# Folding a weight by slices of 120 columns instead of 128, in a linear-attention and gated-unit kernel

## The chip, the cores and the metric

The kernel runs on one core of one Trainium2 chip. The metric is the device time of one execution in microseconds. A profile of one execution comes with each kernel; its times count from the start of the span that the profiler saw.

## What is computed

For 2048 tokens of 640 features, the output is the input plus two branches that both read the normalized input:

```python
xn = layernorm(x)                                    # x: 1 x 2048 x 640
# branch A: linear attention, 32 heads of 20
q, k, v = split(xn @ wqkv)                           # wqkv: 640 x 1920
pq, pk = q @ w_phi[h], k @ w_phi[h]                  # w_phi: 32 x 20 x 20
phi_q = concat(softmax(pq), softmax(-pq))            # likewise phi_k
kv, z = phi_k^T v, sum over tokens of phi_k
a = (phi_q kv / (phi_q z + 1e-6)) @ wo
# branch B: gated unit
b = (silu(xn @ w1) * (xn @ w3)) @ w2                 # w1, w3: 640 x 1536
out = x + a + b
```

Since q @ w_phi = xn @ (wq @ w_phi), the kernel first folds phi into the weights: Wkp = wk @ blockdiag(w_phi), and Wqp = wq @ blockdiag(w_phi). This folding is what the change is about.

## The kernel before

Tokens go in 16 tiles of 128 (T), features in 5 chunks of 128 (DC). The kernel text is not a list of instructions in their final order. Each stage is a generator ("stream") that yields steps: norms, transposes, fold_k, attention (value and key tiles, later the fold of the queries' weights), k_norms, loads, key_values, the query streams, mlps (the gated unit, in 4 blocks of 512 tokens by 12 chunks of 128 hidden features) and outs. A planner, `_Program`, holds a cost for every operation and for every DMA, works out for each stream's next step when it could start, and commits the earliest; ties go by the order of the streams. The order in which it commits the steps is the order on each engine. `commit` holds the costs of DMAs: how long the issuing engine is held (`self.free`) and when the data land (`o.end`). The costs shape the order only, and the waits put into the program are those that the dependencies need. All loads are issued on SyncE (SP), except half of token tile 0, which ScalarE issues.

What matters here:

- `first_loads` issues, in this order: token tiles 0 to 2, wv in two halves, token tile 3, the first third of w1 and w3, phi, the transposed load of wk (640 columns of wqkv into wqkT, 5 chunks of 128), token tiles 4 to 7, tiles 8 to 11.
- `warm_up` lets TensorE multiply zeros at the start, 7 products of 512 columns and 11 of 128.
- `norms` normalizes the token tiles; tiles 0 to 3 are transposed on TensorE, tiles 4 to 15 by transposing DMAs into xnT (`loads`). `loads` also issues the other two thirds of w1 and w3, token tiles 12 to 15 and, after tile 9, the transposed load of wq.
- `block_diag` builds the block-diagonal factor BDc on GpSimd, one product with a mask GM for each chunk. 128 is no multiple of a head's 20, so a chunk holds 7 or 8 heads, of which the first and the last may be cut.
- `fold_mm(which, dc, k)` makes 128 rows of a folded weight: for each of the 5 chunks a product with wqkT as the stationary operand and BDc as the moving one, split where the output passes column 320. The two halves lie in two banks of PSUM, and neighbouring chunks add into the columns of the head that they share. It is evacuated to Wqp or Wkp.
- `attention` runs the value tiles 0 to 3, waits for the fold of wk, and goes on with key tiles and, from tile 4, value tiles. From tile 9 it puts one block of the fold of wq behind each tile.
- Every operation is recorded by a helper, so all of them carry one of two line numbers in the profile (102 for operations, 114 for DMAs). Their tiles tell them apart.

Of the kernel before, what the change touches and what calls it, by code (L numbers as in the profile page):

```python
# [3 lines left out]
ACT = mybir.ActivationFunctionType  # L4
# [5 lines left out]
D = 640  # L10
# [10 lines left out]

ENGINES = ("PE", "ACT", "DVE", "POOL", "SP")
GRAN = 32


def heads_of_chunk(c):
    return (128 * c) // DH, (128 * c + 127) // DH


class _Op:  # L30
# [13 lines left out]
class _Program:  # L44
# [127 lines left out]
    def commit(self, ops):  # L172
        for o in ops:
            o.idx = len(self.ops)
            o.deps = self.find_deps(o)
            t = self.free[o.eng]
            for d in o.deps:
                t = max(t, d.end + 0.07)
            o.start = t
            if o.dma:  # L180
                self.free[o.eng] = t + 0.45
                if "T" == o.part:
                    self.free[o.eng] = t + max(1.3, o.cost / 150e3)
                self.bus = max(self.bus, t + 0.5) + o.cost / (280e3 if o.part else 305e3)
                o.end = self.bus + (1.6 if t < 3.5 else 2.6)
            else:
                o.end = t + o.cost
                self.free[o.eng] = o.end
            self.ops.append(o)
            if o.eng == "POOL" and not o.dma:  # L190
                self.pool = o
            for g in o.reads:
                if isinstance(g, tuple):
                    self.bank.setdefault(g, {})[o.eng] = o
                else:
                    self.last_r.setdefault(g, {})[("dma", o.idx) if o.dma else o.eng] = o
            for g in o.writes:
                if isinstance(g, tuple):
                    self.bank.setdefault(g, {})[o.eng] = o
                else:  # L200
                    self.last_w[g] = o
                    self.last_r.pop(g, None)
# [45 lines left out]
def bass_parallel_sum__linear_kernel_hedgehog__glu_gated_swiglu__prompt_kernel(  # L248
# [29 lines left out]
    def new(name, shape, dtype, offset=None):  # L278
        size = mybir.dt.size(dtype)
        for n in shape[1:]:  # L280
            size *= n
        return P.sbuf(name, shape, dtype, region(size) if offset is None else offset)

    ident = new("ident", [128, 128], bf)
    GM = new("GM", [128, DC, H], bf)
    phi_s = new("phi_s", [128, DC, DH], bf)
    BDc = new("BDc", [128, DC, 8 * DH], bf)
    bst = new("bst", [128, T, 16], f32)
    mv = new("mv", [128, T, 8], f32)
    rstd = new("rstd", [128, T, 8], f32)  # L290
# [36 lines left out]
    oT = new("oT", [128, DC, S], bf, RV)  # L327

    RW = region(12800)
    wqkT = new("wqkT", [128, 2 * DC, D], bf, RW)  # L330
    KVc = new("KVc", [128, H * 21], bf, RW)
    half = new("half", [128, 2, 660], f32, RW + 1408)
    Sq = new("Sq", [128, 4, 72], f32, RW + 6688)
# [53 lines left out]
        copy("ACT" if a <= d else "DVE", o, i, 2 if i.dtype == bf else 1)  # L387

    def memset(eng, o, v):
        P.op(eng, "memset", [o], [], (o, v), cost=0.15 + free(o) / 960)  # L390

    def select(o, base, pattern, cm, cmp, fill):
        P.op("POOL", "affine_select", [o], [o], (),
# [4 lines left out]
    x_t = A_x.rearrange("b (t p) d -> p (b t) d", p=128)  # L398
    out_t = out.rearrange("b (t p) d -> p (b t) d", p=128)
    wqkv_t = A_wqkv.rearrange("(c p) n -> p c n", p=128)  # L400
    phi_t = A_w_phi.rearrange("h d f -> (h d) f").rearrange("(c p) f -> p c f", p=128)
    w1_t = B_w1.rearrange("(c p) f -> p c f", p=128)
    w3_t = B_w3.rearrange("(c p) f -> p c f", p=128)

# [4 lines left out]
    def load_x(a, b):  # L409
        P.dma("SP", x_tok[:, a:b, :], x_t[:, a:b, :])  # L410

    def first_loads():
        def half_wv(a):
            P.dma("SP", wv[:, :, a:a + 320], wqkv_t[:, :, 2 * D + a:2 * D + a + 320])

        P.dma("SP", x_tok[:, 0, 0:320], x_t[:, 0, 0:320])
        P.dma("ACT", x_tok[:, 0, 320:D], x_t[:, 0, 320:D])
        load_x(1, 2)
        load_x(2, 3)
        half_wv(0)  # L420
        half_wv(320)
        load_x(3, 4)
        w13(0, 512)
        P.dma("SP", phi_s[:], phi_t)
        P.dma("SP", wqkT[:, DC:2 * DC, :], A_wqkv[:, D:2 * D], True)
        load_x(4, 8)
        load_x(8, 12)


    def consts():  # L430
        memset("DVE", t1[:, 2, :], 0.0)
        memset("DVE", warm[:], 0.0)
        act(warm[:], warm[:], ACT.Exp)
        memset("POOL", ident[:], 0.0)
        select(ident[:], 0, [[-1, 128]], 1, ALU.not_equal, 1.0)
        memset("POOL", GM[:], 1.0)
        select(GM[:], 0, [[128, DC], [-DH, H]], 1, ALU.is_ge, 0.0)
        select(GM[:], DH, [[-128, DC], [DH, H]], -1, ALU.is_gt, 0.0)
        memset("POOL", mhalf[:], -0.5)

    def consts_late():
# [75 lines left out]


    def block_diag():
        for c in range(DC):  # L520
            h0, h1 = heads_of_chunk(c)
            n = h1 - h0 + 1
            tt("POOL", BDc[:, c, 0:n * DH].rearrange("p (h k) -> p h k", k=DH),
               phi_s[:, c, :].unsqueeze(1).to_broadcast([128, n, DH]),
               GM[:, c, h0:h1 + 1].unsqueeze(2).to_broadcast([128, n, DH]), ALU.mult)

    def fold_mm(which, dc, k):
        first = [True, True]
        for e in range(DC):
            h0, h1 = heads_of_chunk(e)  # L530
            lo, hi = DH * h0, DH * (h1 + 1)
            for q in range(2):
                a, b = max(lo, 320 * q), min(hi, 320 * q + 320)
                if a < b:
                    mm(bank(k + q, b - a, a - 320 * q), wqkT[:, which * DC + e, 128 * dc:128 * dc + 128],
                       BDc[:, e, a - lo:b - lo], first[q], e == DC - 1 or (q == 0 and e == 2), True)
                    first[q] = False
        dst = (Wqp, Wkp)[which]
        evac(dst[:, dc, :].rearrange("p (b c) -> p b c", c=320), bank2(k, 320))


    def proj(t, w, k):
# [177 lines left out]
                       default=0.0)  # L720
        return min((k for k in range(0, 8, n) if k // 2 not in held), key=free_at)

    done = dict.fromkeys(("w", "ln", "t", "f", "k", "n", "kv", "v", "u", "qp", "qn", "qd", "q", "o", "h"), 0)

    def norms():
        yield lambda: (first_loads(), consts())
        yield lambda: act_sum(1, ACT.Copy, bst[:, 1, 0:1])
        yield lambda: (ln_half(0, 0), ln_half(0, 1), ln_rstd(0, 1))
        yield lambda: scalar_op(1, mv[:, 1, 0:1], bst[:, 1, 0:1], -1.0 / D, 0.0)
        yield lambda: act_sum(1, ACT.Square, mv[:, 1, 1:2], mv[:, 1, 0:1])  # L730
        yield lambda: ln_apply(0)
        done["ln"] = 1
        yield lambda: act_rstd(1)
        yield lambda: (ln_half(2, 0), ln_half(2, 1))
        yield lambda: ln_apply(1)
        done["ln"] = 2
        yield lambda: ln_rstd(2, 1)
        yield lambda: ln_half(3, 0)
        yield lambda: ln_apply(2)
        done["ln"] = 3  # L740
        yield lambda: (ln_half(3, 1), ln_rstd(3, 1))
        yield lambda: ln_apply(3)
        done["ln"] = 4
        yield block_diag
        todo = []
        for t in range(4, T + 2, 2):
            if t == T or t > done["k"] + 8 or t == 12 and done["w"] < 8:
                for u in todo:
                    yield lambda u=u: ln_apply(u)
                    done["ln"] = u + 1  # L750
                todo = []
            if t == T:
                break
            while t > done["k"] + 8 or t == 12 and done["w"] < 8:
                yield None
            yield lambda t=t: ln_stats(t, 2)
            for u in todo:
                yield lambda u=u: ln_apply(u)
                done["ln"] = u + 1
            todo = [t, t + 1]  # L760
            if t == 6:
                yield consts_late

    def fold_k():
        for dc in range(DC):
            yield lambda dc=dc: fold_mm(1, dc, banks(2))
        done["f"] += 1
# [22 lines left out]
    def loads():  # L790
        while done["t"] < 4:
            yield None
        for t in range(4, T):
            while done["ln"] <= t:
                yield None
            yield lambda t=t: P.dma("SP", xnT[:, :, t * 128:(t + 1) * 128], x_tok[:, t, :], True)
            done["t"] = t + 1
            if t == 7:
                yield lambda: (w13(512, 1024), load_x(12, 16))
                done["w"] = 8  # L800
            if t == 9:
                yield lambda: w13(1024, 1536)
                done["w"] = 12
                yield lambda: P.dma("SP", wqkT[:, 0:DC, :], A_wqkv[:, 0:D], True)
                done["f"] = 2

    def attention():
# [4 lines left out]
        for t in range(4):  # L812
            while done["t"] <= t:
                yield None
            k = banks(2)
            held.add(k // 2)
            yield lambda t=t, k=k: v_half(t, 0, k)
            while done["t"] < min(t + 2, 4):
                yield None
            yield lambda t=t, k=k: (v_half(t, 1, k), v_store(t, k))  # L820
            held.clear()
        while done["f"] < 1:
            yield None
        for t in range(T):
# [194 lines left out]
```

## Time and profile before

| what | value |
|---|---|
| median of 3 runs | 271.7 us (271.29 to 271.88) |
| profiled execution, its own time | 271.82 us |
| its span | 270.1 us |
| instructions | 4829 |
| TensorE busy | 97% of the span |
| VectorE, ScalarE, GpSimd busy | 66%, 37%, 36% |
| data moved by DMA | 27.73 MB |

PE is TensorE, PEld its weight loads, DVE VectorE, ACT ScalarE, POOL GpSimd, SP SyncE and SPq its queue. In a time line a row reads: start, duration, engine, line, operation, output<-inputs, forms and count, and in brackets the idle time ahead with what ended it. In a table of windows the columns are the stretch, its length, for each engine the busy time and the number of instructions, then TensorE's granted clock, the busy share of the DMA engines, and GB/s.

### The profile page before, as it was taken

The page shows a single profiled execution, that of the slowest core. Times are in us where ns is not written, and L with a number is a line of the kernel's source. Part 1 is how long each engine was busy: PE and PEld are TensorE (multiplying, and loading weights), DVE is VectorE, ACT ScalarE, POOL GpSimd, SP SyncE. Part 2 cuts the span into 40 slices and gives each one's busy share as a digit, 9 for nine tenths or more (in the row PEclk, how much of TensorE's full clock was granted, in tenths as well). Part 3 has the DMA queues.
Part 4 walks back from the last instruction along what each step waited for, and adds up shares of the span by engine and source line. Part 5 has one row for each costly group of instructions (what it writes and reads, how often), then busy time and mean ns, then how long its engine had stood idle before and what let it go on. Part 6 is the DMA issues. An engine that isn't in the chain of part 4 may idle for free.

```text
span 270.1 us, 4829 instructions
## 1 busy us (share of the span) xinstructions
PE 263.2 (97%) x1959; PEld 161.4 (60%) x1979; DVE 177.7 (66%) x306; ACT 100.9 (37%) x194; POOL 97.5 (36%) x126
## 2 busy tenths in 40 slices
PE   7999999999999999999999999999999999999996
PEld 4556666677845555454554554554577777777774
DVE  4459899999898988777798777797734121212112
ACT  5567995988446242434333433423100000000000
POOL 4317589889994444213444224443200000000000
PEclk9999999999999999999999999999999999999999
DMA  7981699850097352344451344422454323131211
GB/s 187 304 243 24 154 291 295 113 151 2 9 333 98 61 104 48 59 78 80 78 45 40 73 80 79 78 23 58 102 71 127 82 72 97 51 97 49 88 36 49
DMA packets 63510, 27.73 MB, mean 103 GB/s; under 512 B 49792, under 2 KB 63488, under 8 KB 63488
## 3 DMA queue, kind: packets, MB, share of 16 engines
q1 hardware_dynamic: 63344, 27.35, 44.8%
q8 instruction: 15, 0.25, 0.4%
q10 hardware_dynamic: 144, 0.08, 0.2%
q14 instruction: 7, 0.06, 0.1%
HBM read 12.81 MB, written 2.62 MB: 57 GB/s over the span
## 4 chain that ended last, share of the span: by engine, by line
PE 69%; DVE 10%; POOL 7%; DMA 4%; ACT 4%; issue 3%; SPq 2%; DVEq 0%
PE PS L102 69%; POOL ekt L102 6%; DMA wqkT<-in_A_wqkv_dram 4%; DVE S L102 3%; ACT ekt L102 2%; SPq L114 2%; DVE t L102 1%; DVE rS L102 1%; DVE Sq L102 1%; POOL rstd L102 1%; DVE hT L102 1%; DVE bst L102 1%; DVE rq L102 1%; ACT x_tok L102 1%; DVE x_tok L102 1%
## 5 line engine op out<-in xcount | busy, mean ns | idle before, releaser
L102 PE MATMUL PS<-xnT,w_s 128*128 128x512 bf16 x463 | 105.1, 379 | 1.1
L102 PEld LDWEIGHTS PS<-xnT,w_s 128*128 128x128 bf16 x480 | 45.4, 98 | 50.0 <-ACT Wkp L102 0.3
L102 PE MATMUL PS<-w_s,hT 128*128 128x320 bf16 (+2 forms) x384 | 54.9, 299 | 0.0
L102 DVE TENSOR_TENSOR xres<-PS,xres 128x640 bf16<-128x640 f32 (+2 forms) x17 | 13.4, 786 | 57.4 <-PE PS L102 57.4
L102 POOL TENSOR_TENSOR eq<-eq,rq 128x600 bf16<-128x600 bf16 (+1 forms) x32 | 22.7, 731 | 73.4 <-DVE rq L102 73.3
L102 PEld LDWEIGHTS PS<-w_s,hT 128*128 128x128 bf16 x384 | 37.6, 98 | 14.6
L102 ACT ACTIVATE th<-PS 128x512 f32<-128x512 f32 x48 | 28.7, 599 | 46.4 <-PE PS L102 46.4
L102 DVE SCALAR_TENSOR_TENSOR t<-th,PS 128x512 bf16<-128x512 f32 x48 | 32.6, 679 | 20.2 <-ACT th L102 20.2
L102 POOL TENSOR_TENSOR ekt<-ekt,rS 128x640 bf16<-128x640 bf16 x32 | 39.6, 1280 | 5.1 <-DVE rS L102 5.1
L102 ACT ACTIVATE eq<-PS 128x600 bf16<-128x600 f32 (+1 forms) x72 | 24.8, 412 | 29.8 <-PE PS L102 29.7
L102 DVE SCALAR_TENSOR_TENSOR hT<-t,PS 128x512 bf16<-128x512 bf16 x48 | 33.0, 687 | 1.7
L102 PE MATMUL PS<-wv,xnT 128*128 128x320 bf16 x160 | 24.8, 299 | 0.5 <-ACT xnT L102 0.3
L102 ACT ACTIVATE ekt<-PS 128x640 bf16<-128x640 f32 x32 | 22.4, 704 | 7.1 <-PE PS L102 6.5
L102 PE MATMUL PS<-wo_s,oT 128*128 128x320 bf16 (+2 forms) x160 | 24.5, 299 | 0.0
L102 PE MATMUL PS<-Wqp,xnT 128*128 128x512 bf16 (+1 forms) x157 | 23.7, 297 | 0.5 <-DVE t L102 0.3
L102 PE MATMUL PS<-Wkp,xnT 128*128 128x320 bf16 x160 | 23.9, 299 | 0.1
L102 DVE TENSOR_REDUCE S<-ekt 128x64 f32<-128x1280 bf16 x16 | 23.0, 1438 | 0.0
L102 PEld LDWEIGHTS PS<-Wqp,xnT 128*128 128x128 bf16 x160 | 13.3, 98 | 12.3 <-DVE t L102 0.5
L102 PEld LDWEIGHTS PS<-wv,xnT 128*128 128x128 bf16 x160 | 15.2, 98 | 7.2 <-ACT xnT L102 1.4
L102 PEld LDWEIGHTS PS<-Wkp,xnT 128*128 128x128 bf16 x160 | 15.4, 98 | 6.5 <-ACT ekt L102 0.3
L102 POOL TENSOR_TENSOR half<-eq 128x660 f32<-128x660 bf16 x14 | 19.0, 1359 | 0.5 <-ACT eq L102 0.5
L102 PEld LDWEIGHTS PS<-wo_s,oT 128*128 128x128 bf16 x160 | 15.5, 98 | 6.1
(56 smaller groups left out, 177.7 us busy)
## 6 DMA issues: line engine op xcount, KB each, us to landing
w_s<-in_B_w_dram SPq DMA_DIRECT2D x6, 640.0 KB, 6.6
xres<-in_A_x_dram SPq DMA_DIRECT2D x16, 160.0 KB, 2.4
out_dram<-xres SPq DMA_DIRECT2D x15, 160.0 KB, 1.8
x_tok<-in_A_x_dram SPq DMA_DIRECT2D x3, 640.0 KB, 6.2
w_s<-in_B_w_dram SPq DMA_DIRECT2D x1, 1920.0 KB, 8.2
wv<-in_A_wqkv_dram SPq DMA_DIRECT2D x2, 400.0 KB, 4.7
wo_s<-in_A_wo_dram SPq DMA_DIRECT2D x1, 800.0 KB, 4.8
x_tok<-in_A_x_dram SPq DMA_DIRECT2D x3, 160.0 KB, 3.3
```

The source lines that it names most:

```text
L102: o = _Op(eng, lambda: m(*args, **kw), r, w, cost)
L114: o = _Op(eng, lambda: m(out, in_), self.regions(in_), self.regions(out), nbytes, True)
```

## The change

Weight columns are taken in slices of 120 (six heads), five of them, and a sixth of 40 (two heads). No head is cut any more, so slices do not add into each other's columns, and a block of the fold takes six products (five of 120 columns and one of 40) in place of four of 140 and two of 80. Each slice is loaded by a transposed load of its own, 128 columns wide for the first five and 64 for the last, into the tile wT. The output of a block lies in 640 adjoining columns over the border of two banks. The block-diagonal factor BD is made by two instructions. phi comes in two loads, the small one issued by ScalarE. Token tiles 4 to 7 are loaded ahead of wk. A few constants are set later, and some of the planner's cost figures for DMAs and memsets are different.

```diff
@@ commit
-                self.free[o.eng] = t + 0.45
+                self.free[o.eng] = t + (0.45 if o.cost > 5e4 or o.eng == "ACT" else 1.6)
                 if "T" == o.part:
-                    self.free[o.eng] = t + max(1.3, o.cost / 150e3)
+                    self.free[o.eng] = t + max(1.45 if t < 20 else 1.3, o.cost / 150e3)
                 self.bus = max(self.bus, t + 0.5) + o.cost / (280e3 if o.part else 305e3)
-                o.end = self.bus + (1.6 if t < 3.5 else 2.6)
+                o.end = max(self.bus, t + 1.45 if o.part else 0) + (1.6 if t < 3.5 else 2.6)
@@ tiles
-    GM = new("GM", [128, DC, H], bf)
-    phi_s = new("phi_s", [128, DC, DH], bf)
-    BDc = new("BDc", [128, DC, 8 * DH], bf)
+    GM = new("GM", [128, 6], bf)
+    phi_s = new("phi_s", [128, 6, 32], bf)
+    BD = new("BD", [128, 6, 120], bf)
...
-    wqkT = new("wqkT", [128, 2 * DC, D], bf, RW)
+    wT = new("wT", [128, 6, D], bf, RW)
@@ loads
+    def load_wT(which):
+        for g in range(6):
+            n = 128 if g < 5 else 64
+            a = D * which + 120 * g
+            P.dma("SP", wT[0:n, g, :], A_wqkv[:, a:a + n], True)
@@ first_loads
         P.dma("ACT", x_tok[:, 0, 320:D], x_t[:, 0, 320:D])
+        P.dma("ACT", phi_s[0:40, 5, 0:DH], phi_t[600:D, :])
...
-        P.dma("SP", phi_s[:], phi_t)
-        P.dma("SP", wqkT[:, DC:2 * DC, :], A_wqkv[:, D:2 * D], True)
+        P.dma("SP", phi_s[0:120, 0:5, 0:DH], phi_t[0:600, :].rearrange("(c p) f -> p c f", p=120))
         load_x(4, 8)
+        load_wT(1)
         load_x(8, 12)
@@ block_diag
-        for c in range(DC):
-            h0, h1 = heads_of_chunk(c)
-            n = h1 - h0 + 1
-            tt("POOL", BDc[:, c, 0:n * DH].rearrange("p (h k) -> p h k", k=DH), ...
+        for n, a, b in ((120, 0, 5), (40, 5, 6)):
+            m = n // DH
+            o = BD[0:n, a:b, 0:n].rearrange("p c (h f) -> p c h f", f=DH)
+            tt("POOL", o, phi_s[0:n, a:b, 0:DH].unsqueeze(2).to_broadcast([n, b - a, m, DH]),
+               GM[0:n, 0:m].unsqueeze(1).unsqueeze(3).to_broadcast([n, b - a, m, DH]), ALU.mult)
@@ fold_mm
-        first = [True, True]
-        for e in range(DC):
...
-        dst = (Wqp, Wkp)[which]
-        evac(dst[:, dc, :].rearrange("p (b c) -> p b c", c=320), bank2(k, 320))
+        c0 = k * 512 + 152
+        for g in range(6):
+            n = 120 if g < 5 else 40
+            mm(PS[:, c0 + 120 * g:c0 + 120 * g + n], wT[0:n, g, 128 * dc:128 * dc + 128], BD[0:n, g, 0:n],
+               g in (0, 3), g in (2, 5), True)
+        evac((Wqp, Wkp)[which][:, dc, :], PS[:, c0:c0 + D])
@@ fold_k: waits until block_diag is committed
+        while not done["bd"]:
+            yield None
@@ loads, after tile 9
-                yield lambda: P.dma("SP", wqkT[:, 0:DC, :], A_wqkv[:, 0:D], True)
+                yield lambda: load_wT(0)
@@ norms, attention: consts_late moves from behind tile 6's statistics to behind value tile 3
```

More of the change, by code (lines that the diff above doesn't have):

```diff
@@ L23 @@
 GRAN = 32
-def heads_of_chunk(c):
-    return (128 * c) // DH, (128 * c + 127) // DH
 class _Op:
@@ L389, in memset @@
     def memset(eng, o, v):
-        P.op(eng, "memset", [o], [], (o, v), cost=0.15 + free(o) / 960)
+        P.op(eng, "memset", [o], [], (o, v), cost=0.15 + free(o) / (960 if free(o) < 512 or eng == "DVE" else 230))
     def select(o, base, pattern, cm, cmp, fill):
@@ L400, in bass_parallel_sum__linear_kernel_hedgehog__glu_gated_swiglu__prompt_kernel @@
     wqkv_t = A_wqkv.rearrange("(c p) n -> p c n", p=128)
-    phi_t = A_w_phi.rearrange("h d f -> (h d) f").rearrange("(c p) f -> p c f", p=128)
+    phi_t = A_w_phi.rearrange("h d f -> (h d) f")
     w1_t = B_w1.rearrange("(c p) f -> p c f", p=128)
@@ L436, in consts @@
         memset("POOL", GM[:], 1.0)
-        select(GM[:], 0, [[128, DC], [-DH, H]], 1, ALU.is_ge, 0.0)
-        select(GM[:], DH, [[-128, DC], [DH, H]], -1, ALU.is_gt, 0.0)
+        select(GM[:], 0, [[-DH, 6]], 1, ALU.is_ge, 0.0)
+        select(GM[:], DH, [[DH, 6]], -1, ALU.is_gt, 0.0)
         memset("POOL", mhalf[:], -0.5)
@@ L519, in block_diag @@
     def block_diag():
-        for c in range(DC):
-            h0, h1 = heads_of_chunk(c)
-            n = h1 - h0 + 1
-            tt("POOL", BDc[:, c, 0:n * DH].rearrange("p (h k) -> p h k", k=DH),
-               phi_s[:, c, :].unsqueeze(1).to_broadcast([128, n, DH]),
-               GM[:, c, h0:h1 + 1].unsqueeze(2).to_broadcast([128, n, DH]), ALU.mult)
-    def fold_mm(which, dc, k):
-        first = [True, True]
-        for e in range(DC):
[L530 to L537, printed above, removed]
-        dst = (Wqp, Wkp)[which]
-        evac(dst[:, dc, :].rearrange("p (b c) -> p b c", c=320), bank2(k, 320))
+        for n, a, b in ((120, 0, 5), (40, 5, 6)):
[3 more added lines that the diff above has]
+               GM[0:n, 0:m].unsqueeze(1).unsqueeze(3).to_broadcast([n, b - a, m, DH]), ALU.mult)
+    def fold_mm(which, dc, k):
+        c0 = k * 512 + 152
[4 more added lines that the diff above has]
+        evac((Wqp, Wkp)[which][:, dc, :], PS[:, c0:c0 + D])
     def proj(t, w, k):
@@ L721, in banks @@
         return min((k for k in range(0, 8, n) if k // 2 not in held), key=free_at)
-    done = dict.fromkeys(("w", "ln", "t", "f", "k", "n", "kv", "v", "u", "qp", "qn", "qd", "q", "o", "h"), 0)
+    done = dict.fromkeys(("w", "ln", "t", "f", "k", "n", "kv", "v", "u", "qp", "qn", "qd", "q", "o", "h", "bd"), 0)
     def norms():
@@ L744, in norms @@
         yield block_diag
+        done["bd"] = 1
         todo = []
@@ L760, in norms @@
             todo = [t, t + 1]
-            if t == 6:
-                yield consts_late
     def fold_k():
+        while not done["bd"]:
+            yield None
         for dc in range(DC):
@@ L821, in attention @@
             held.clear()
+        yield consts_late
         while done["f"] < 1:
```

## The prediction

> **What bounds the kernel now.** I read the page first: its busy shares and the chain of work that ended last.
>
> ```profile
> span 270.1 us, 4829 instructions
> PE 263.2 (97%) x1959; PEld 161.4 (60%) x1979; DVE 177.7 (66%) x306; ACT 100.9 (37%) x194; POOL 97.5 (36%) x126
> PE   7999999999999999999999999999999999999996
> PE 69%; DVE 10%; POOL 7%; DMA 4%; ACT 4%; issue 3%; SPq 2%; DVEq 0%
> ```
>
> TensorE is busy for 263.2 of 270.1 us, in all slices but the first and the last. So the kernel is bound by TensorE nearly everywhere: work taken off other engines gains nothing, while a wait put into TensorE's queue lengthens the run by its full length, because hardly any idle time (6.9 us in all) is there to swallow it. Next comes the place that the diff touches. The chain of waits, in order of time, holds this passage:
>
> ```profile
> 5.18 1.02 SPq L114
> ...
> 6.25 10.53 DMA wqkT<-in_A_wqkv_dram
> 16.78 0.14 issue
> 16.91 0.49 PE PS L102 x6
> ```
>
> and the time lines of TensorE and of SyncE's queue show what stands around it and around the second fold:
>
> ```profile
> 14.39 2.10 PE L102 MATMUL PS<-xnT,w_s 128*128 128x512 bf16 x9
> 16.91 1.76 PE L102 MATMUL PS<-BDc,wqkT 128*128 128x140 bf16 x30 [0.41 <-DMA wqkT<-in_A_wqkv_dram]
> 18.78 2.33 PE L102 MATMUL PS<-xnT,w_s 128*128 128x512 bf16 x10
> 20.95 5.60 PE L102 MATMUL PS<-Wkp,xnT 128*128 128x320 bf16 x40
> ...
> 47.21 2.10 PE L102 MATMUL PS<-xnT,w_s 128*128 128x512 bf16 x9
> 49.15 0.48 PE L102 MATMUL PS<-BDc,wqkT 128*128 128x140 bf16 x6
> 49.47 1.52 PE L102 MATMUL PS<-Wkp,xnT 128*128 128x320 bf16 x10
> ```
>
> ```profile
> 5.18 1.02 SPq L114 DMA_DIRECT2D phi_s<-in_A_w_phi_dram  x1
> 6.25 6.97 SPq L114 DMA_TRANSPOSE wqkT<-in_A_wqkv_dram  x1
> 13.27 1.12 SPq L114 DMA_DIRECT2D x_tok<-in_A_x_dram  x2
> ...
> 37.11 2.00 SPq L114 DMA_DIRECT2D w_s<-in_B_w_dram  x2
> 39.15 6.46 SPq L114 DMA_TRANSPOSE wqkT<-in_A_wqkv_dram  x1
> 45.65 6.43 SPq L114 DMA_TRANSPOSE xnT<-x_tok  x4
> ...
> DMA to landing us min/median/max: 8.7/9.6/10.5
> ```
>
> The first transposed load lands 10.53 us after its issue, at 16.78, and TensorE waits 0.41 us for it. The second is issued at 39.15 and lands 8.7 us later, at 47.85; the first fold of the queries' weights begins at 49.15, so that load has 1.3 us to spare. Both are tight: whatever makes them later is paid for.
>
> **The step that decides: the sixth slice.** The changed program's list of instructions, as built, has these lines on SyncE:
>
> ```
> DMACopy x_tok<-in_A_x_dram 128x4x640
> DmaTransposeAnt wT<-in_A_wqkv_dram 128x640 x5
> DMACopy wT<-in_A_wqkv_dram 64x640x1
> DMACopy x_tok<-in_A_x_dram 128x4x640
> ```
>
> Five slices go out as hardware transposes. The sixth is only 64 columns wide, and it has become a plain copy with a transposing access pattern: neighbours in a destination row are 1920 elements apart in the source, so each 2-byte element is a run of its own, 64 x 640 = 40,960 of them. The same line stands in the second load. Over 16 engines that is 2560 packets for each engine, on the queue that all of SyncE's transfers share. What one costs the trace does not show, since it has no transfer of 2-byte runs. It bounds it:
>
> ```profile
> DMA packets 63510, 27.73 MB, mean 103 GB/s; under 512 B 49792, under 2 KB 63488, under 8 KB 63488
> ...
> q1 hardware_dynamic: 63344, 27.35, 44.8%
> ...
> DMA packets 1133, 0.29 MB, mean 290 GB/s; under 512 B 1133, under 2 KB 1133, under 8 KB 1133
> ...
> 17.00:18.00 1.00, 1.00 (x21) 1.00 (x21) 0.50 (x1) 0.58 (x1) 0.00 (x0) 1.00 1.04 381
> ```
>
> The first two rows are of the whole run. The third is the microsecond from 13 to 14, in which the queue carries the first transposed load alone: 1133 packets of 256 bytes on 16 engines, 14.1 ns a packet. The last is a microsecond of wide loads at 381 GB/s, 0.042 ns a byte and engine, by which 256 bytes take 10.7 ns; the other 3.4 ns belong to the packet as such.
> - Lower end: only the 3.4 ns count. 2560 x 3.4 ns = 9 us for the copy.
> - Middle: a packet costs what the smallest packet seen in bulk costs. 2560 x 14.1 ns = 36 us.
> - Upper end by the issue: the load of phi, 640 runs of 40 bytes, held SyncE for 1.02 us, 1.6 ns a run; 40,960 x 1.6 ns = 65 us.
> - Upper end by the mean packet: 44.8% of 16 x 270.1 us over 63,344 packets is 30.6 ns; x 2560 = 78 us.
>
> I take 36 us, call it C, because it stands on the row nearest in kind: the same matrix, the same queue, the same source stride, packets that are small. The Trainium skill (DMA: Bandwidth & Descriptors, Rules for kernel authors) says that a non-contiguous last dimension lowers to one descriptor per element and should be avoided; no run yet shows it here.
>
> **First fold.** SyncE's order is now phi, tiles 4-7, five transposes, the copy. The five transposes cover as many 128x128 blocks as before (25), so their issue costs the same 7.0 us; one load of four tiles (half of 1.12 us) comes ahead of it, and its 0.66 MB at 381 GB/s take 1.7 us of the queue. The five slices therefore land near 16.8 + 1.7 = 18.5, and the copy's packets, which follow them, at 18.5 + C. TensorE's new order puts two gated-unit blocks ahead of the fold (20 matmuls in place of 10): one takes 20.95 - 18.78 = 2.2 us, so it reaches the fold at 14.4 + 4.4 = 18.8. Five of six products of the first block can run; the sixth waits for the copy. TensorE executes in order, so all is queued behind it: the fold, two more blocks, the key tiles. ScalarE has the evacuations of Wkp next, and behind them the normalization of tiles 4 and 5; SyncE's later entries (tiles 8-11, all transposes of xnT, the rest of w1 and w3) lie behind the copy in the same queue. Stall: 18.5 + 36 - 18.8, about 36 us.
>
> **Second fold.** The same transfers stand between the folds as before: four xnT transposes, w1 and w3, x, two xnT, w1 and w3. So the distance in time stays about what it was, the five transposes would again land 1.3 us early, and the copy makes that C - 1.3 too late. The transposes of tiles 10 to 15 now lie behind it: at 6.43 us for four, the first needs 1.6 us more of issue, where it lay as close behind before. Key tile 10 follows the fold at once, so about a microsecond of that shows. Stall: about 36 us.
>
> **TensorE after a stall.** No gap of TensorE in this trace is longer than 1.24 us, but its start shows what cold work costs:
>
> ```profile
> 1.24 4.24 PE L102 MATMUL PS<-t 128*128 128x512 bf16 x18 [1.24 <-DVE warm L102]
> ```
>
> These are 7 products of 512 columns and 11 of 128, 4992 columns in 4.24 us. The key tiles from 20.95 to 26.59 do 40 x 320 columns in 5.64 us, 2270 a microsecond, at which 4992 would take 2.2 us. So a cold start loses 2.0 us; twice that, 4 us (0 to 4). The Trainium skill (TensorE: Matmul & The Clock Gate, Rules for kernel authors) says that an idle gap of over about 3 us halves the clock; the start above agrees in size.
>
> **What the change saves.** Each block of the fold has 640 columns in six products, where it had four of 140 and two of 80, 720 in all. Ten blocks save 800 columns, 0.35 us at 2270 a microsecond. The old wait of 0.41 us goes, since it is part of the new one. The mask product on GpSimd becomes 600 and 40 elements in place of five instructions:
>
> ```profile
> 12.54 1.97 POOL L102 TENSOR_TENSOR BDc<-phi_s,GM 128x140 bf16<-128x140 bf16 x5 [1.86 <-DMA phi_s<-in_A_w_phi_dram]
> L102 POOL TENSOR_TENSOR half<-eq 128x660 f32<-128x660 bf16 x14 | 19.0, 1359 | 0.5 <-ACT eq L102 0.5
> ACT t L102 <- DMA x_tok<-in_A_x_dram: 0.9, 1, 0.9
> ```
>
> 660 elements take 1.36 us there, so the product ends near 12.5 + 1.6 = 14.1, long before the fold at 18.8: nothing on the path. The extra small load on ScalarE's queue costs an issue of some 0.4 us at the start, inside the 0.9 us in which ScalarE waits for x; were that cover gone, it would cost those 0.4 us. The constants set later, the other cost figures of the planner and the single evacuation of 640 adjoining columns only move work that TensorE's queue hides.
>
> **Sum**, against the profiled execution, 271.8 us (span 270.1 and 1.7 around it; the median of the runs is 271.7): 271.8 + 36 + 36 + 4 - 0.4 - 0.35 = 347 us. In general it is 275 + 2C: 293 for 9 us, 405 for 65 us, 431 for 78 us.
>
> **Rivals.**
> - *The descriptors are the limit, not the packets.* The generator that feeds the queue needs 1.6 ns for each run, as for phi, and C is 65 us: 405 us. For it: the issue of phi, 25 KB, is nearly twice as long as that of a load of four token tiles (half of 1.12 us). Against: phi may have waited for the 1.3 MB of w1 and w3 ahead of it. Chance 0.28.
> - *The copy is far cheaper than its packets say.* The Trainium skill (VectorE: DVE Perf Modes, The three transpose paths) gives 19 times the time of the hardware transpose for a strided copy, for a large innermost stride in the destination, which this copy does not have. As a mechanism of this kernel, runs are merged on the way: at 290 GB/s the 82 KB would take 0.28 us, 19 times that is 5.4 us, stalls of 5.1 and 4.1 us, a microsecond for xnT and up to 4 of cold clock: about 285 us. For it: the destination rows are contiguous. Against: 40,960 elements in 5.4 us are 2.1 ns for each on an engine, less than the 3.4 ns that a packet costs beside its bytes. Chance 0.08.
> - *Faster.* The sixth slice lands with the other five, within 0.3 us, as it would if it were a small transpose: no stall at either fold, TensorE goes on at 18.8, and the 0.41 us and the 0.35 us are gained: 271.0 us. It decides where C is under about 0.3 us at the first fold and 1.3 us at the second. For it: 82 KB is half a slice. Against: the row of 1133 packets in a microsecond, by which 40,960 of any size take 36. Chance 0.04.
>
> **How the numbers follow.** The forecast, C between 13 and 55 us, has 0.60; the rivals have 0.28, 0.08 and 0.04. The predicted time is 347 us. The range reaches to the rival of the descriptors and to the mean packet, and leaves out the merged runs, the faster case, and a little of each end: 298 to 425 us. Faster by over 0.2% (the least that a measurement of this kernel tells from no change) needs the third rival: 0.02. Within 0.2%, the same case with the gain spent elsewhere: 0.02. Slower: 0.96.
>
> **What would show it.** In the profile of the changed kernel, TensorE's waits would be led by the load of wT, two waits of tens of microseconds, one near 19 us and one some 28 us after the first ends; the strip of 40 slices would show two holes in TensorE, with DMA engines busy at almost no GB/s; packets would rise by about 81,900, from 63,510 to some 145,000. If SyncE's issue of the copy takes about as long as its landing, descriptors were the limit; if it is short, packets were. I am wrong if the packets do not rise, if TensorE waits under 3 us for wT at either fold, or if the two stalls differ by more than a quarter.

## The result and the profile after

The changed kernel takes 379.88 us (median of 4 runs, 379.02 to 380.17) against 271.5 us for the kernel before in the same comparison: a ratio of 1.3998, 95% interval 1.3975 to 1.4022. The profiled execution took 380.17 us, with a span of 378.4 us, 108.3 us more than before.

The head of the page, with the strips of 40 slices (a slice is 9.5 us):

```profile
span 378.4 us, 4860 instructions
PE 270.8 (72%) x1979; PEld 164.2 (43%) x1979; DVE 172.6 (46%) x305; ACT 102.1 (27%) x195; POOL 96.8 (26%) x123
...
PE   7900000399800000899999999999999999999997
...
PEclk9965555599965555699999999999999999999999
DMA  7999999959999999700833532242443343322221
GB/s 237 212 7 2 2 2 2 70 147 269 126 2 2 2 2 15 179 0 2 260 62 73 95 74 57 55 57 56 86 83 58 74 74 87 88 69 74 79 76 35
DMA packets 145727, 27.90 MB, mean 74 GB/s; under 512 B 132009, under 2 KB 145705, under 8 KB 145705
```

TensorE has two holes of five slices each. While they last, the DMA engines are busy throughout and move 2 GB/s. The packets rose by 82,217; two copies of 40,960 runs are 81,920. TensorE's waits, and its time line around the two folds:

```profile
PE PS L98 <- DMA wT<-in_A_wqkv_dram: 102.8, 4, 51.9
...
PE PS L98 <- DMA xnT<-x_tok: 0.4, 1, 0.4
```

```profile
18.87 0.23 PE L98 MATMUL PS<-BD,wT 120*128 120x120 bf16 x1 [0.29 <-DMA wT<-in_A_wqkv_dram]
19.93 0.21 PE L98 MATMUL PS<-BD,wT 120*128 120x120 bf16 x1 [0.83 <-DMA wT<-in_A_wqkv_dram]
72.00 3.25 PE L98 MATMUL PS<-BD,wT 40*128 40x40 bf16 x25 [51.85 <-DMA wT<-in_A_wqkv_dram]
75.17 5.33 PE L98 MATMUL PS<-xnT,w_s 128*128 128x512 bf16 x20
80.34 6.96 PE L98 MATMUL PS<-Wkp,xnT 128*128 128x320 bf16 x50
...
152.28 0.21 PE L98 MATMUL PS<-BD,wT 40*128 40x40 bf16 x1 [49.78 <-DMA wT<-in_A_wqkv_dram]
152.85 2.82 PE L98 MATMUL PS<-Wkp,xnT 128*128 128x320 bf16 x10 [0.35 <-DMA xnT<-x_tok]
155.47 2.87 PE L98 MATMUL PS<-wv,xnT 128*128 128x320 bf16 x10
158.13 0.83 PE L98 MATMUL PS<-BD,wT 120*128 120x120 bf16 x6
158.90 1.53 PE L98 MATMUL PS<-Wkp,xnT 128*128 128x320 bf16 x10
```

Both long waits end at the 40-row product, the one that reads the sixth slice. After each, products run at about half their pace for a while: a pair of key and value tiles takes 2.82 and 2.87 us where it takes 1.5 each otherwise. SyncE's queue shows the copies, what waited behind them, and, in its last line, how long the loads of wT took to land, the copies being the longest:

```profile
8.41 9.58 SPq L110 DMA_TRANSPOSE wT<-in_A_wqkv_dram  x5
18.04 0.73 SPq L110 DMA_DIRECT2D wT<-in_A_wqkv_dram  x1
18.82 47.84 SPq L110 DMA_DIRECT2D x_tok<-in_A_x_dram  x1
76.06 5.20 SPq L110 DMA_TRANSPOSE xnT<-x_tok  x4
...
98.60 0.63 SPq L110 DMA_DIRECT2D wT<-in_A_wqkv_dram  x1
99.28 55.66 SPq L110 DMA_TRANSPOSE xnT<-x_tok  x6
...
DMA to landing us min/median/max: 3.1/5.2/53.9
```

The copy itself is issued in 0.73 us, but the load behind it holds SyncE for 47.84 us. In the microsecond from 40 to 41 the DMA queue shows

```profile
DMA packets 799, 0.00 MB, mean 2 GB/s; under 512 B 799, under 2 KB 799, under 8 KB 799
...
q1 hardware_dynamic: 799, 0.00, 195.2%
```

799 packets a microsecond on 16 engines are 20.0 ns a packet; 2560 of them are 51.3 us. The copy did not start at that pace. From 20 to 21 us the queue carried

```profile
DMA packets 2497, 0.00 MB, mean 5 GB/s; under 512 B 2497, under 2 KB 2497, under 8 KB 2497
```

which is 6.4 ns a packet; 1381 packets followed in the next microsecond, and from 22 to 68 us about 798 in each. So 20.0 ns is the lasting pace of 2-byte runs, reached after some 4000 packets. What lets the first ones through faster, and what then holds the others, no run here tells.

### The profile page after: what moved, and what is told of

It reads as the page before. It is cut to its first block, busy times and chain, and to the rows that moved or that the text cites. A ratio compares the mean times of both kernels' runs of the same rounds, so it can differ in the third digit from the quotient of the medians.

```text
span 378.4 us, 4860 instructions
## 1 busy us (share of the span) xinstructions
PE 270.8 (72%) x1979; PEld 164.2 (43%) x1979; DVE 172.6 (46%) x305; ACT 102.1 (27%) x195; POOL 96.8 (26%) x123
## 4 chain that ended last, share of the span: by engine, by line
PE 67%; another core or an unknown queue 27%; SPq 4%; DMA 1%; issue 0%; DVE 0%
PE PS L98 67%; SPq L110 4%; DMA wT<-in_A_wqkv_dram 1%; DVE xres L98 0%
## 5 line engine op out<-in xcount | busy, mean ns | idle before, releaser
L98 PE MATMUL PS<-xnT,w_s 128*128 128x512 bf16 x480 | 109.0, 381 | 0.0
L98 PE MATMUL PS<-BD,wT 120*128 120x120 bf16 (+1 forms) x60 | 7.1, 250 | 102.8 <-DMA wT<-in_A_wqkv_dram 102.8
L98 PEld LDWEIGHTS PS<-BD,wT 120*128 120x128 bf16 (+1 forms) x60 | 5.2, 114 | 105.5 <-DMA wT<-in_A_wqkv_dram 102.4
L98 DVE BATCH_NORM_STATS2 bst<-x_tok 128x6 f32<-128x320 bf16 x30 | 14.0, 482 | 54.3 <-DMA x_tok<-in_A_x_dram 53.8
L98 PE MATMUL PS<-wv,xnT 128*128 128x320 bf16 x160 | 26.1, 310 | 0.5 <-ACT xnT L98 0.3
L98 PE MATMUL PS<-Wkp,xnT 128*128 128x320 bf16 x160 | 25.0, 310 | 0.4 <-DMA xnT<-x_tok 0.4
```

What stands on the lines that cost most here:

```text
L98: o = _Op(eng, lambda: m(*args, **kw), r, w, cost)
```

## The experiments

The theory is that the two copies of 2-byte runs are the whole loss, each by a stall of its own. The rivals are that other parts of the change carry much of it, and, for the length of a copy, that the generation of descriptors, the steps in the source, the bytes, or the destination set it. Each edit is against the changed kernel unless it says otherwise. Kernels without an interval ran once.

**Both sixth slices by hardware transposes** (`e1_all_hw`)

```diff
-            n = 128 if g < 5 else 64
+            n = 128
```

> Both sixth slices are loaded 128 columns wide, so that they go out as hardware transposes; all else of the change stays. Theory (the copy of 2-byte runs is the whole loss): no wait of tens of microseconds is left; the sixth transpose adds one more issue of 1.3 to 1.9 us behind the fifth, which landed at 19.8 us, so the first fold waits some 2 to 3 us and the second up to 1 us: 272 to 275 us. Rival (other parts of the change, its order of loads or the narrower products, carry a good part of the 108 us): above 285 us.

275.66 us, 1.0148 (1.0122 to 1.0174) of the kernel before. 104 of the 108 us go with a change of one number. The rest of the change is still a loss of 4.0 us, and the time is 0.7 us above the upper end expected; the last four kernels are about that.

**One at a time** (`e2_first_hw`, `e3_second_hw`)

```diff
+            n = 128 if g < 5 or which == 1 else 64    # e2: the copy of wq stays
+            n = 128 if g < 5 or which == 0 else 64    # e3: the copy of wk stays
```

> Only the sixth slice of the first load (wk) goes out as a hardware transpose; that of the second (wq) stays a copy. Theory (each copy is a stall of its own at its own fold, some 50 us of waiting and 2 to 3 us of cold clock): about 271 + 2 + 53 = 326 us, with one hole in TensorE, of which the start moves from 102 to about 50 us. Rival (the two are coupled, for instance the second stalls only because the first shifted the queues): under 300 us or over 350 us.

> Only the sixth slice of the second load (wq) goes out as a hardware transpose; that of the first stays a copy. Theory of two separate stalls: about 271 + 54 + 1 = 326 us with one hole from 20 to 72 us. Rival (coupled): under 300 us or over 350 us.

327.45 and 328.04 us, with one hole each. Over the 275.66 us of `e1_all_hw` these are 51.8 and 52.4 us, together 104.2, the whole difference between 275.66 and 379.88. The stalls add, and neither makes the other.

**40 columns** (`e4_40_columns`)

```diff
-            n = 128 if g < 5 else 64
+            n = 128 if g < 5 else 40
```

> The sixth slice has 40 columns in place of 64, which is all that the fold reads: 25,600 runs of 2 bytes in place of 40,960. 40 rows do not divide over 16 engines; if the transfer is dealt by whole equal shares it goes to 10 engines, 2560 runs each, as many for each engine as before. Theory P (an engine's packets are the limit, 20 ns each): the copy keeps its length, 51 us, and the kernel about 380 us. Theory G (the generator of descriptors is the limit, 51.3 us over 40,960, 1.25 ns each, for all engines together): 32 us for the copy and about 380 - 2 x 19 = 342 us. If the rows are spread over all 16 engines (2 or 3 rows each, 1920 packets at most), P gives 38 us and about 354 us.

380.53 us: 37.5% fewer elements, no shorter copy. From 40 to 41 us:

```profile
DMA packets 497, 0.00 MB, mean 1 GB/s; under 512 B 497, under 2 KB 497, under 8 KB 497
...
q1 hardware_dynamic: 497, 0.00, 121.3%
```

The busy share fell from 195.2 to 121.3%, by 10/16: ten engines work, each at the same pace of 20.1 ns. So no generator common to all engines sets the length, since it would have fed ten engines faster; what counts is the packets on an engine.

**A near source** (`e6_near_source`)

```diff
-                P.dma("SP", wT[0:n, g, :], A_wqkv[:, a:a + n], True)
+                # sixth slice only; issued as a plain copy
+                P.dma("SP", wT[0:n, g, :], A_wqkv[64 * which:64 * which + 64, 0:1280].rearrange("p (c two) -> p c two", two=2)[:, :, 0], "plain")
```

> The sixth slice is again a plain copy of 40,960 runs of 2 bytes into the same 64 rows, but it reads every second element of 64 rows of wqkv, so that neighbouring runs lie 4 bytes apart in the source and not 3840. (The values that land there are other weights than the fold asks for.) 40 columns left a packet at 20 ns on its engine with 10 engines at work. Theory R (the far steps in the source make it 20 ns, against the 14.1 ns of a 256-byte packet): a packet falls to some 7 to 14 ns, the copy to 18 to 36 us, the kernel to about 312 to 349 us. Theory W (20 ns is what a 2-byte packet costs, wherever it is read): unchanged, about 380 us.

379.85 us, and 798 packets in the same microsecond. Steps of 4 bytes in the source cost as much as steps of 3840, so the far steps were not the reason.

**Runs of 4 bytes** (`e7_pairs`)

```diff
-                P.dma("SP", wT[0:n, g, :], A_wqkv[:, a:a + n], True)
+                # sixth slice only; issued as a plain copy
+                P.dma("SP", wT[0:n, g, :], A_wqkv[0:320, a:a + 128].rearrange("r (p two) -> p r two", two=2), "plain")
```

> The sixth slice is a plain copy of the same number of bytes from the same columns of wqkv, but in runs of 4 bytes, two neighbouring elements each: 64 rows of 320 runs, 1280 packets for each engine in place of 2560, with the same 3840-byte steps in the source. (The values land in another order than the fold asks for.) Theory W (each packet costs 20 ns whatever its size): half the copy, 25.6 us, about 380 - 2 x 25.6 - 1 = 328 us. Rival (bytes, or 4-byte runs cost twice as much): near 380 us.

300.55 us, 27 us less than the theory of a fixed price had it. TensorE's first wait is 12.49 us in place of 51.85. Two microseconds of the first copy, from 20 to 21 and from 24 to 25:

```profile
DMA packets 2295, 0.01 MB, mean 9 GB/s; under 512 B 2295, under 2 KB 2295, under 8 KB 2295
...
DMA packets 1705, 0.01 MB, mean 7 GB/s; under 512 B 1705, under 2 KB 1705, under 8 KB 1705
```

That is 7.0 and 9.4 ns a packet. The first lies in a quick start like that of the 64-column copy, which carried 2497 packets in such a microsecond; the second is the lasting pace (1701 to 1706 packets in each microsecond from 23 to 29). At the lasting pace there are half the packets at less than half the price of each: a run of 2 bytes (20.0 ns) is dearer than one of 4, and dearer than the 14.1 ns of a 256-byte packet of the transposes.

**48 and 32 columns** (`e5_48_columns`, `e11_32_columns`)

```diff
+            n = 128 if g < 5 else 48                              # e5
+            # e11, sixth slice only:
+                P.dma("SP", wT[0:32, g, :], A_wqkv[:, a:a + 32], True)
+                P.dma("SP", wT[32:64, g, :], A_wqkv[32:64, 0:D])
```

> The sixth slice as a copy of 48 columns: 30,720 runs of 2 bytes on 16 engines, 1920 for each. Theory W with the limit on each engine: 1920 x 20 ns = 38.4 us, so about 380 - 2 x 12.8 = 354 us. Rival (a copy of 2-byte runs has a length of its own that does not follow the count on an engine): 380 us as with 64 and with 40 columns.

> 48 columns were slower than 64 and not faster: 480 packets a microsecond in place of 798, while 40 columns (10 engines) gave 498. Here the copy has 32 columns, 20,480 runs of 2 bytes, 2 rows for each of 16 engines; rows 32 to 63 of the slice are filled by one wide plain load, so eight of the fold's columns get other weights. The planner now puts two more gated-unit blocks ahead of the first fold, 4.4 us of cover. Theory D (the limit lies at the destination: each group of four rows takes a 2-byte write every 20 to 25 ns, and engines that share a group share that): 8 groups, 320 to 400 packets a microsecond, 51 to 64 us for each copy, the kernel at 372 to 400 us, no faster than with twice the elements. Theory E (each engine's packets are the limit at 20 ns, and 48 rows were slow for another reason): 798 a microsecond, 26 us for each copy, about 322 us.

48 columns took 402.37 us, worse than 64, which neither theory had. 32 columns took 325.69 us. From 40 to 41 us, the first view is of 48 columns, the second of 32:

```profile
DMA packets 496, 0.00 MB, mean 1 GB/s; under 512 B 496, under 2 KB 496, under 8 KB 496
...
q1 hardware_dynamic: 496, 0.00, 196.7%
```

```profile
DMA packets 800, 0.00 MB, mean 2 GB/s; under 512 B 800, under 2 KB 800, under 8 KB 800
```

With two rows for each engine (32), as with four (64 on 16, 40 on 10), a packet takes 20 ns. Theory D, which gave at most 400 a microsecond for 32 columns, falls. With 48 columns the busy share, 196.7%, is that of 16 engines, so each had three rows, and a packet takes 32 ns. Why, stays open: three rows, or the way in which 48 rows fall on the engines, were not told apart.

**What the other 4 us are: the order of loads** (`e8_order_alone`, against the kernel before; `e9_hw_old_order`, against `e1_all_hw`)

```diff
         # e8, in the kernel before
-        P.dma("SP", wqkT[:, DC:2 * DC, :], A_wqkv[:, D:2 * D], True)
         load_x(4, 8)
+        P.dma("SP", wqkT[:, DC:2 * DC, :], A_wqkv[:, D:2 * D], True)
         # e9, in e1_all_hw
-        load_x(4, 8)
         load_wT(1)
+        load_x(4, 8)
```

> The kernel before with one edit: token tiles 4 to 7 are loaded ahead of the transposed load of wk. That load's packets then follow 0.66 MB more, 1.7 us at 381 GB/s, so the first fold waits about 2.1 us in place of 0.4, unless the planner puts the second gated-unit block ahead of it, which covers 2.2 us. Theory (the order of loads is most of the 4 us by which the version with six hardware transposes is slower than before): 273 to 275 us. Rival (the order costs nothing, and the six separate transposes with their longer issue and the changed order of steps cost the 4 us): 271 to 272 us.

> All slices by hardware transposes, but with wk loaded ahead of token tiles 4 to 7, as before the change. Theory (the order of loads is most of the 4 us): 271 to 272.5 us. Rival (the six transposes and the changed order of steps are): still 274 to 276 us.

The order alone: 1.0003 (0.9994 to 1.0011), no change; there, too, the planner put two gated-unit blocks ahead of the fold, which then waited 0.55 us for wk. The old order in the version with hardware transposes: 275.86 us, 1.0168 (1.0132 to 1.0203). The order of loads is not the cause of the 4 us, and that theory falls.

**Partial height** (`e10_full_height`, against `e1_all_hw`)

```diff
+        memset("POOL", phi_s[:], 0.0)                 # ahead of its loads
...
-            tt("POOL", o, phi_s[0:n, a:b, 0:DH]. ...  # rows 0 to n of BD
+            tt("POOL", o, phi_s[:, a:b, 0:DH]. ...    # all 128 rows
...
-            mm(..., wT[0:n, g, 128 * dc:128 * dc + 128], BD[0:n, g, 0:n], ...)
+            mm(..., wT[:, g, 128 * dc:128 * dc + 128], BD[:, g, 0:n], ...)
```

> The version with six hardware transposes, with the stationary operands of the fold 128 rows high in place of 120 and 40: phi is zeroed first and the rows beyond a slice's heads are zeros in BD, so the result is the same and the columns and the banks of the output stay. phi's small load moves to SyncE, ahead of token tiles 4 to 7. Theory (partial height makes the fold slow: a block of six products took 0.48 us there, from 49.39 to 49.87, where the old six products with 80 more columns took 0.32 us): a block of the second fold takes 0.27 to 0.32 us, and the kernel gains 10 x 0.16 = 1.6 us, less some 0.5 us for the extra issue: 274 to 275 us. Rival (the layout over the border of two banks, or the six separate outputs make it slow): the block stays at 0.48 us and the kernel at 275.5 us or more.

A block of the second fold with hardware transposes, first with partial, then with full height:

```profile
49.39 0.55 PE L98 MATMUL PS<-BD,wT 120*128 120x120 bf16 x6
49.87 1.53 PE L98 MATMUL PS<-Wkp,xnT 128*128 128x320 bf16 x10
```

```profile
50.77 0.45 PE L98 MATMUL PS<-BD,wT 128*128 128x120 bf16 x6
51.06 1.52 PE L98 MATMUL PS<-Wkp,xnT 128*128 128x320 bf16 x10
```

Start to start, 0.48 us became 0.29. So partial height is what makes the narrower products slower than the wider ones were, and layout is not. Whether the time lies in the products or in their loads of weights is not shown: the loads of 120 rows and of 128 have the same mean, 97 ns, in the two traces. For ten blocks the gain is 1.9 us. But the kernel took 274.77 us, 1.0132 (1.0111 to 1.0154), 0.9 us less than `e1_all_hw`, and the two ratios overlap. TensorE's wait for the evacuation of Wkp and a table of windows, both of the full-height version, show what worked against the gain in the profiled execution:

```profile
PE PS L98 <- ACT Wkp L98: 2.6, 3, 1.8
```

```profile
25.00:28.00 3.00, 0.89 (x7) 0.31 (x5) 2.49 (x7) 2.84 (x5) 1.39 (x5) 1.00 0.58 114
28.00:30.00 2.00, 2.00 (x10) 1.21 (x10) 2.00 (x3) 0.71 (x2) 1.88 (x4) 0.60 0.60 130
30.00:32.00 2.00, 2.00 (x10) 1.16 (x8) 2.00 (x2) 0.77 (x2) 0.88 (x1) 0.54 1.06 359
32.00:34.00 2.00, 2.00 (x17) 1.44 (x15) 1.93 (x5) 1.97 (x3) 0.88 (x1) 1.00 1.04 322
```

TensorE, done sooner with the fold, waited longer for ScalarE's evacuation of Wkp (2.6 us in all; 1.9 with partial height), was busy for only 0.89 of 3 us, and the granted clock then fell to 0.60 and 0.54: ten products of 320 columns in 2 us instead of 17. The 46 key products from 27.89 us on took 7.94 us, where the trace of `e1_all_hw`, in which the clock stayed at 1.00, has 6.26. This drop is no mark of full height, though. It is some 1.7 us of clock, 0.6% of the span, and the mean granted clock of each execution shows whether it had one: 0.994 in three of the four with full height (274.69 to 275.02 us) and 0.993 or 0.994 in three of the five of `e1_all_hw` (275.66 to 275.97), 1.000 in the others (274.22, and 274.75 and 275.50). So at a like clock full height is some 0.9 us ahead, in few executions; of the rest of the 1.9 us, the longer wait explains 0.7, and what is left is open.

**Full height and the old order** (`e12_full_height_old_order`)

```diff
         # in e10_full_height
-        load_x(4, 8)
         load_wT(1)
+        load_x(4, 8)
```

> Six hardware transposes, full-height stationary operands, and wk loaded ahead of token tiles 4 to 7 as before the change: the best of the parts seen so far. With full height, a block of the second fold took 0.29 us (50.77 to 51.06), yet the kernel gained only 0.9 us, with a passage of 46 key products at 7.9 us in place of 6.3. If the waits for the evacuation of Wkp that came ahead of that passage go with the old order: 272.5 to 273.5 us. If they stay: 274 to 276 us. In either case the sixth transpose, 1.3 us more of issue on each load, keeps it at or above the kernel before.

275.37 us, 1.0137 (1.0104 to 1.0170): the waits only changed their place. In the trace, which is of an execution of 277.02 us, they are:

```profile
PE PS L98 <- DMA wT<-in_A_wqkv_dram: 2.4, 3, 1.1
PE PS L98 <- DMA xnT<-x_tok: 1.8, 3, 0.9
```

Here the second fold waits for the longer transposed load, the first key tile after four for xnT, and the granted clock was 0.50 from 56 to 58 us. Three of the six executions had a mean clock of 0.994 and took 276.19 to 277.02 us; the other three, at 1.000, took 274.25 to 274.55, which is still above the longest of the kernel before, 272.02. None of these versions beats the kernel before. The trace of `e1_all_hw` has these waits of TensorE:

```profile
PE PS L98 <- ACT Wkp L98: 1.9, 3, 1.3
...
PE PS L98 <- ACT v L98: 0.9, 1, 0.9
```

For the 4.0 us of `e1_all_hw`, it gives 1.6 us of slower folds (ten blocks at 0.48 in place of 0.32), 1.9 us of waits for the evacuation of Wkp and 0.9 us for one of v, less the old wait of 0.4. That sum is an account from the rows; only its first term was tested by itself, and without it the kernel gained 0.9 us, which is not clear of the noise.

## Why the prediction was right

**What bounds the kernel.** Right. TensorE had no room for a wait: the 102.8 us of waiting for wT stand in a span longer by 108.3 us, and the two copies, taken away one at a time, add up to the 104.2 us that both cost together.

**The sixth slice.** Right in kind: 82,217 more packets, two holes, each ended by the product that reads the sixth slice. The Trainium skill's rule (DMA: Bandwidth & Descriptors, Rules for kernel authors) of one descriptor for each element of a non-contiguous last dimension agrees: 81,920 were worked out.

**Its price, C.** This term was mis-sized: 36 us expected, 51.3 us by the packet rate. The failed step is "a packet costs what the smallest packet seen in bulk costs". I took the price of 256-byte packets, which by my own split is mostly a price of bytes, for 2-byte ones; at the lasting pace a 2-byte run costs 20.0 ns, a 4-byte run 9.4 ns, 256 bytes 14.1 ns. Size was not the scale, and nothing in the trace of before could show that 2 bytes stand apart. The 51.3 us lie inside the 13 to 55 us of the forecast, near their end (55 us is 385 us by 275 + 2C): the width of the interval covered them, not the row on which 36 us stood. The dearest price that I had, 30.6 ns from the busy share, was not sound: the share counts packets that overlap. In the copy it is 195.2% of 16 engines for 799 packets, 39.1 ns a packet, while the packets follow each other on an engine after 20.0 ns.

**The first stall** was expected at C: 52.97 us came (0.29, 0.83 and 51.85). **The second** was also expected at about C, because the same transfers lie between: 50.13 us (49.78 and 0.35). They start at 20.1 us and 30.5 us after the first ended (near 19, and 28, expected). That the five transposes cost the same issue as the one before did not hold: they took 9.58 us where 7.0 was expected, and the waits of 0.29 and 0.83 us came for slices among them.

**Cold clock.** 4 us expected. After the first stall, the rest of the fold and two gated-unit blocks took 8.34 us (72.00 to 80.34); at the full pace of `e1_all_hw` and of before they take about 24 x 0.08 + 4.34 = 6.3, a loss of 2.1. After the second, 152.28 to 158.90 is 6.62 us, of which 0.35 is a wait; the next such group, 158.90 to 162.11, takes 3.21, and the single product before it some 0.1, a loss of about 3.0. Together 5.1 us, above the 0 to 4 us allowed. The strip PEclk goes down to 0.5 in both holes, and after the first the granted clock was still 0.50 from 72 to 76 us; the trace of before had no hole to show it. So the Trainium skill's rule on idle gaps that the prediction names (on that page it stands in the section Why this matters for your kernels) agrees with this trace.

**Savings.** Wrong in sign: 0.35 us of gain was expected from 80 fewer columns a block. Six products of partial height take 0.48 us where the wider full ones took 0.32, so the fold costs 1.6 us more. Small beside 104, it is the 1.6 in the account of the 4.0 us that are left without the copies.

**The sum** with measured terms: 271.8 + 53.0 + 50.1 + 5.1 + 1.6 - 0.4 = 381.2 against 380.17 for the profiled execution.

**The rivals.** The descriptor rival stood nearer in time (405 us) but its mechanism fell: 25,600 runs on ten engines took as long as 40,960 on sixteen. The sign I had given for it, how long the copy's own issue lasts, told nothing, since the queue took the copy in 0.73 us and held the next load instead. The merged runs (285 us) fell with the packet count. The 19 times of a hardware transpose that the Trainium skill (VectorE: DVE Perf Modes, The three transpose paths) gives for a strided copy is stated for a large innermost stride in the destination, which this copy does not have, and it is far too little here: an estimate by the 290 GB/s of the transposes, 0.28 us for these bytes, makes it 51.3 / 0.28, some 180 times. The faster case did not come, and it would not have come with a hardware transpose either: that is 275.66 us, not 271.0. There the step that failed is that a sixth transpose lands with the other five at no cost and that narrower products are shorter.

## What to carry to other kernels

Read the built instruction list, not only the source: a call named for a transpose became an element-by-element copy when a slice was 64 columns wide and not 128, and on a kernel bound by TensorE with everything in one DMA queue that cost 52 us each time. Asking for more data than needed (128 columns for 40) took 104 us off. And count the rows of a stationary operand, not only the columns of the moving one: padding with zero rows to 128 made a group of six products 0.19 us shorter, of which the whole kernel showed 0.9 us for ten groups, not clear of the noise.

## What the runs showed of the hardware that was not expected

- DMA runs of 2 bytes settle at 20.0 ns each on their engine, with source steps of 4 bytes as of 3840 (798 and 799 packets a microsecond), after a first microsecond at 6.4 ns (2497 packets). Runs of 4 bytes settle at 9.4 ns (1705), after a start at 7.0 (2295).
- A copy to 40 destination rows had 10/16 of the busy share of one to 64 rows (121.3 and 195.2%), so 10 of 16 engines, and took as long. One to 48 rows, three for each engine, took 32 ns a packet and longer than 64; not explained.
- Six products with 120 and 40 rows took 0.48 us, with 128 rows 0.29, at the same 640 columns.
- The granted clock fell to 0.50 in the holes of 50 us, and, in some executions of kernels without such holes, to 0.60 and 0.54 after 3 us in which TensorE was busy for 0.89 and its longest single wait was 1.82 us.
